# Requests for three of the four w_in pieces moved behind the first parting of the queries

## The chip, the cores and the metric

The kernel runs on one core of one Trainium2 chip. The metric is the device time of one execution in microseconds (us); lower is better. A time is the median of several executions. A profile is one more execution, recorded by the hardware profiler, with times counted from the start of its span.

## What is computed

Two blocks follow one another. The first is a gated linear attention with 4 batches, 8 heads, 768 tokens and 48 numbers a head. The second is a feed-forward block on 3072 tokens of width 384, with a hidden width of 1024, a softmax-weighted activation and a layer norm.

```python
for t in range(S):
    state = alpha[:, :, t, :, None] * state + np.einsum('bhd,bhe->bhde', k[:, :, t], v[:, :, t])
    y[:, :, t] = np.einsum('bhd,bhde->bhe', q[:, :, t], state)
...
h = x @ w_in
e = np.exp(h - h_max)
solu = h * (e / (np.sum(e) + 1e-09))
ln = (solu - mean) / np.sqrt(var + 1e-06) * g_ln
return ln @ w_out
```

The two weight matrices w_in (384 x 1024) and w_out (1024 x 384) arrive as 64-bit floats. The kernel brings their raw words into SBUF and makes 32-bit floats of them itself.

## The kernel before, in words

The tokens are worked on in six groups of 128 tokens of each of the four batches. For each group there is an attention part (turn alpha, keys and queries so that a head's numbers lie on partitions; scan alpha for the decays; scale keys and queries; scores; mask; read the values into y) and a feed-forward part (eight slices of the hidden width: `up_mm`, L390 to L398, multiplies x by a slice of w_in into a tile h; `up_act`, L400 to L413, takes the exponential on ScalarE, the product on VectorE and a square on ScalarE; `down`, L507, multiplies by w_out).

The schedule is written out by hand: every engine executes its instructions in the order in which the program text issues them. From the second group on, attention and feed-forward work of neighbouring groups are interleaved. The change is in the stretch ahead of that, which prepares group 0 (L674 to L780) and has no earlier group to lie beside.

What is issued there, by queue:

- **SP (SyncE)** requests by DMA, in this order: alpha (L674), k and q (L682, L683), each in two DMAs of 384 KB made of rows of 192 bytes; v (`load_v`, L173) in four of 192 KB; then w_in. The later w_out, k, q and alpha requests of the loop at L753 follow on the same queue. SP's requests share a fixed set of completion semaphores, so that a request can wait for the landing of the one eight places earlier.
- **w_in** comes in four pieces of 256 columns. `fetch` (L573 to L589) issues three DMAs a call, one for each 128 rows of w_in (L584). `fetch(0, 3)` brings the first piece (three of 256 KB) into slot 3 of the tile `room`, `fetch(1, 4)` the second (three of 256 KB) into slot 4, and `fetch(2, 1, 2)` the third and fourth together (three of 512 KB) into slots 1 and 2. `room` is 9216 columns wide, in six slots of 1536; later the products u and w_out pieces use it too.
- **VectorE (DVE)** turns a piece into 32-bit floats in five steps (`bit`, L613 to L636; the last, L636, writes w_in or w_out). The first piece is converted behind the masks of group 0 (`bits(0)`, L739), the second at L744, the third and fourth and all of w_out in the loop at L753, between the products at L409.
- **ScalarE** copies turned tiles, checks the raw pieces (`in_range`, L596 to L607) and parts the queries: `apart` (L243) takes the queries' last 16 dimensions, which lie in pairs of heads, and writes them twice, once multiplied by a column `parity` that is 1 on the even head's rows and once by its opposite. These are two instructions (L245), the first for even heads, the second for odd ones.
- **TensorE** turns alpha, k and q by matmuls with the identity (L164), computes the scores (`scores`, L271, matmuls at L278), in two halves of four heads; within a half first the first 32 dimensions of its heads, then the last 16 of the even heads, then those of the odd ones, which need the second instruction of `apart`. DVE (L289) and ScalarE with GpSimd (L297, L298) mask them. `read_values` (L356, matmuls at L333) then reads the values into y, batch after batch; ScalarE copies y to x (L363); `keys_back` (L300, L303) turns the keys back; and the loop at L753 begins with the first h (L394). `warm` (L449) fills TensorE with idle matmuls at the start and while q is awaited.

`apart` has three callers: L731 for group 0, L811 for group 1, and L899 for the others.

Of the kernel before, what the change touches and what calls it, by code (L numbers as in the profile page):

```python
# [32 lines left out]
def fast_path(ctx, tc, q, k, v, alpha, moe_w_in, moe_w_out, moe_g_ln, out):  # L33
# [12 lines left out]
    nc = tc.nc  # L46
# [34 lines left out]
    parity = const.tile([P, 2], FP, name="parity")  # L81
# [9 lines left out]
    slots = [room[:, 1536 * i : 1536 * i + 1536] for i in range(6)]  # L91
# [123 lines left out]
    def scan_on(g, i):  # L215
        part = slice(NP * i, NP * i + NP)
        scan(aT[:, part], aT[:, part], seed[:, part], False)
# [22 lines left out]
        copy(out=qe[:, :, P:SW], in_=h4[:, H:NB, 1:2])  # L240
        copy(out=qv[:, 0:H, P:SW], in_=h4[:, 0:H, 1:2])

    def apart():  # L243
        for i in range(2):
            nc.scalar.mul(  # L245
                out=qv[:, H : 2 * H, 0:P].rearrange("p (j i) t -> p j i t", i=2)[:, :, i], in_=qe[:, :, 0:P],
                mul=parity[:, i : i + 1],
            )
# [22 lines left out]
    def scores(g, half, a=None):  # L271
        a = a or banks("a", [NP, P])
        for last in range(2):
            for i in (0, 2, 1, 3):
                h = half * NP + i
                kb, qb = (H + h // 2, H + h) if last else (h, h)
                for b in range(B):
                    nc.tensor.matmul(  # L278
                        a[b][:, i], lhsT=kT[quarter(b), kb], rhs=qv[quarter(b), qb, 0:P], start=not last and not i, stop=bool(last),
                        tile_position=(32 * b, 0), skip_group_check=True,  # L280
                    )
        masks[half] = a
# [290 lines left out]
    def fetch(i, slot, n=1):  # L573

        kind, f = pieces[i]
        w = n * F // (2 if kind else KC)
        raw = room[:, 1536 * slot : 1536 * (slot + n)].bitcast(U32).rearrange("p (c f w) -> p c f w", f=w, w=2)
        if kind:
            parts = [(slice(0, P), c, moe_w_out[(f + c) * P : (f + c + 1) * P, :]) for c in range(2)]
        else:  # L580
            parts = [(slice(0, P), c, moe_w_in[c * P : (c + 1) * P, f * P : f * P + w]) for c in range(KC)]
        for rows, c, src in parts:
            if float64:
                nc.sync.dma_start(out=raw[rows, c].rearrange("p f w -> p (f w)"), in_=src.bitcast(U32))  # L584
            else:
                dst = w_out[rows, f + c, 0:DM] if kind else w_in[rows, c, f * P : f * P + w]
                nc.sync.dma_start(out=dst, in_=src)
        for m in range(n):
            raws[i + m] = raw[:, :, w // n * m : w // n * (m + 1)]  # L589
# [101 lines left out]
    nc.gpsimd.memset(kg, 0.0)  # L691
    load_v(0)
    fetch(0, 3)
    fetch(1, 4)
    fetch(2, 1, 2)
    nc.vector.memset(ones, 1.0)
    nc.vector.memset(small_ones, 1.0 / 32)
    nc.vector.memset(mhalf, -0.5)
    nc.vector.memset(w_out[:, :, DM : DM + 1], 1.0)

    def three(name, where):
        return [pool.tile([P, NP, P], FP, tag=tag, name=f"{name}{i}") for i, (pool, tag) in enumerate(where)]
# [20 lines left out]
    for i in (0, 2, 1):  # L723
        if i == 1:
            scan_on(0, i)
        part = slice(NP * i, NP * i + NP)
        nc.vector.tensor_tensor(
            out=qe[:, :, 0:P] if i == 2 else qv[:, part, 0:P], in0=t[i], in1=aT[:, part, 1:SW], op=ALU.mult
        )
        if i == 2:  # L730
            apart()  # L731
    scores(0, 0)
    t = [x.tile([P, NP, P], FP, tag=n, name="a_" + n) for x, n in ((ps_h, "h"), (ps_o, "o")) for _ in range(2)]
    scores(0, 1, t)
# [74 lines left out]
    scan_on(1, 2)  # L809
    nc.vector.tensor_tensor(out=qe[:, :, 0:P], in0=tq[2], in1=aT[:, H:NB, 1:SW], op=ALU.mult)  # L810
    apart()  # L811
    ends_of_decay()
    move_lasts()
# [56 lines left out]
    def attend(a, what):  # L870
# [19 lines left out]
        elif what == "firsts":  # L890
# [5 lines left out]
            if more:  # L896
                load(q, qn, a + 1)
        elif what == "apart":
            apart()  # L899
        elif what == "decay":  # L900
            decay(a)
# [89 lines left out]
    def compare(out, x, bound, op):  # L991
# [6 lines left out]
        out=chunks[:, :, 2], in0=sums[:, :, 2], scalar=0.25, in1=sums[:, :, 3], op0=ALU.mult, op1=ALU.is_le  # L998
# [6 lines left out]
    else:  # L1005
# [9 lines left out]
        out=bad, in0=all_ok[0:1, 0:1], scalar1=float(P * ends[-1]), scalar2=None, op0=ALU.is_lt  # L1015
# [415 lines left out]
def kernel(tc, *args):  # L1431

    with ExitStack() as ctx:
        taken = fast_path(ctx, tc, *args)
    with tc.If(taken > 0):
        general_path(tc, *args)
# [30 lines left out]
```

## Time and profile before

| | us |
|---|---|
| three executions without profile, median | 366.96 (366.78 to 367.19) |
| the profiled execution | 368.38 |
| its span, first to last instruction | 366.6 |
| TensorE busy in the span | 358.0 |
| VectorE busy | 243.9 |
| ScalarE busy | 146.5 |
| GpSimd busy | 130.3 |

The granted TensorE clock was 0.998. Of the 366.6 us, the first 28 us prepare and read group 0; the first h starts at 29.64, and from about 97.6 us on attention and feed-forward work alternate.

How to read the views. The page names an engine's busy time and its share of the span; a line of forty digits gives the busy tenths of forty equal slices. In timeline rows the columns are start, length, engine, line, operation, output and inputs, shape, count, and in brackets the idle time just before with what ended it; "issue" means that the profile shows nothing that the instruction waited for. A table of waits gives for each instruction and releaser the total, the number of times and the longest. A table of stretches gives for each stretch its length, busy time and instructions of TensorE's matmuls, TensorE's weight loads, VectorE, ScalarE and GpSimd, then the granted clock, the DMA share and GB/s. In DMA views q1 is the queue of SP's requests and q8 a queue of kind "instruction". A 32-bit matmul appears as two records, each with a weight load of its own.

The main times of the stretch that the change touches:

| what | start, us |
|---|---|
| SP requests v, four DMAs | 11.36, 12.87, 13.63, 15.24 |
| SP requests the first piece of w_in | 16.26, 16.94, 17.42 |
| SP requests the second piece | 17.90, 18.37, 18.85 |
| SP requests the third and fourth | 19.35, 21.11, 21.73 |
| scores of the first half begin | 17.73 |
| the two instructions of `apart` | 18.31, ending 19.65 |
| first y matmul | 22.26 |
| DVE's first conversion step, first piece | 24.15 |
| the same, second piece | 28.56 |
| first h | 29.64 |
| DVE's first conversion step, third piece | 33.66 |
| next SP request (w_out) | 31.58 |

### The profile page before, as it was taken

Reading aid. Unit: us, or ns where it says so; the run is one execution under the profiler, and the core shown is the slowest. Engines: PE = TensorE matmul, PEld = TensorE weight load, DVE = VectorE, ACT = ScalarE, POOL = GpSimd, SP = SyncE. Lnnn points to the kernel's source line nnn. Section 1 sums busy time; section 2 is a strip of 40 time slices with the busy share of each in tenths; the row PEclk is TensorE's granted clock in tenths of the full one; section 3 lists DMA queues with packets and bytes.
Section 4 is the critical chain, followed back from the end, with each engine's and each line's share of the span. In section 5 each row is a group of like instructions: output and inputs, shape, how many; then the busy total and the mean of one; then the engine's idle time right before and its main releaser. Section 6 shows DMA issues by size and latency. Waiting matters only on the chain. (4 is left out here: it accounts for less than half of the span.)

```text
span 366.6 us, 10041 instructions
## 1 busy us (share of the span) xinstructions
PE 358.0 (98%) x4341; PEld 216.0 (59%) x4341; DVE 243.9 (67%) x375; ACT 146.5 (40%) x262; POOL 130.3 (36%) x127
## 2 busy tenths in 40 slices
PE   8989999999999999999999999999999999999994
PEld 8866345666655566556475556575556565555552
DVE  0999989979997796936665946766946404445420
ACT  3637887372736261252531253531242222222110
POOL 7020000003368663764232763332773121233300
PEclk9999999999999999999999999999999999999999
DMA  9994997326196509354044454004042000000011
GB/s 178 186 333 139 194 302 156 88 59 146 68 222 133 131 4 192 90 123 123 5 108 92 103 115 113 21 25 88 21 96 66 0 25 1 23 21 22 23 46 51
DMA packets 72871, 36.06 MB, mean 98 GB/s; under 512 B 48232, under 2 KB 70000, under 8 KB 72816
## 3 DMA queue, kind: packets, MB, share of 16 engines
q1 hardware_dynamic: 71792, 34.39, 39.6%
q10 hardware_dynamic: 1024, 0.92, 0.8%
q8 instruction: 36, 0.59, 0.7%
q14 instruction: 19, 0.16, 0.1%
HBM read 25.30 MB, written 4.72 MB: 82 GB/s over the span
## 5 line engine op out<-in xcount | busy, mean ns | idle before, releaser
L513 PE MATMUL o<-w_out,room 128*128 128x385 f32 x384 | 133.8, 491 | 0.0
L394 PE MATMUL h<-x,w_in 128*128 128x512 f32 x288 | 131.6, 597 | 0.0
L513 PEld LDWEIGHTS o<-w_out,room 128*128 128x128 f32 x384 | 71.1, 189 | 55.2 <-issue 13.4
L394 PEld LDWEIGHTS h<-x,w_in 128*128 128x128 f32 x288 | 53.2, 189 | 58.0 <-issue 49.0
L409 DVE TENSOR_TENSOR room<-h,e 128x512 f32<-128x512 f32 x40 | 27.6, 690 | 72.7 <-ACT e L408 72.7
L408 ACT ACTIVATE e<-h 128x512 f32<-128x512 f32 x40 | 23.9, 598 | 98.9 <-PE h L394 98.9
L427 POOL TENSOR_TENSOR p<-p,e 128x512 f32<-128x512 f32 x30 | 43.1, 1437 | 20.3 <-ACT e L408 20.2
L412 ACT ACTIVATE u<-room 128x512 f32<-128x512 f32 x40 | 25.2, 630 | 37.0 <-DVE room L409 37.0
L552 POOL TENSOR_TENSOR r<-sums,mhalf 128x1 f32<-128x1 f32 x20 | 14.8, 740 | 67.9 <-DVE sums L543 67.7
L289 DVE TENSOR_TENSOR sT<-a,mask 128x512 f32<-128x512 f32 x43 | 26.7, 682 | 8.7 <-PE a L278 8.7
L204 DVE TENSOR_TENSOR_SCAN hT<-aT,unit 128x516 f32<-128x516 f32 x18 | 24.3, 1396 | 7.9 <-ACT aT L709 7.8
L204 DVE TENSOR_TENSOR_SCAN aT<-aT,seed 128x516 f32<-128x516 f32 x18 | 25.4, 1441 | 0.2
L225 POOL TENSOR_TENSOR kT<-kT,hT 128x1024 f32<-128x1024 f32 (+1 forms) x8 | 13.3, 1687 | 33.6 <-DVE kT L179 33.6
L278 PEld LDWEIGHTS a<-qv,kT 32*128 32x128 f32 x704 | 21.1, 186 | 6.8 <-issue 2.4
L427 DVE TENSOR_TENSOR p<-p,u 128x512 f32<-128x512 f32 x30 | 21.7, 723 | 5.1 <-ACT u L412 5.1
L333 PE MATMUL y<-sT,vn 128*32 128x128 f32 x768 | 23.3, 274 | 1.6 <-issue 1.4
L278 PE MATMUL a<-qv,kT 32*128 32x128 f32 x704 | 23.7, 279 | 0.2 <-ACT qv L245 0.2
L212 POOL COPY fend<-hT 128x12 f32<-128x12 f32 x6 | 3.0, 507 | 56.4 <-DVE hT L204 56.4
L333 PEld LDWEIGHTS y<-sT,vn 128*32 128x32 f32 x768 | 20.9, 110 | 3.5 <-issue 2.7
L196 ACT ACTIVATE sq<-an,mone 128x1536 uint8<-128x1536 f32 x12 | 18.9, 1572 | 0.2
L554 ACT ACTIVATE o_sb<-o,r 128x384 f32<-128x384 f32 x16 | 9.3, 580 | 18.5 <-POOL r L552 18.5
L261 POOL TENSOR_TENSOR state<-state,lot 128x384 f32<-128x384 f32 x10 | 8.8, 902 | 15.6 <-DMA lot<-qv 15.6
(150 smaller groups left out, 376.7 us busy)
## 6 DMA issues: line engine op xcount, KB each, us to landing
vn<-in_v_dram SPq DMA_DIRECT2D x24, 192.0 KB, 4.7
an<-in_alpha_dram SPq DMA_DIRECT2D x20, 192.0 KB, 4.0
out_dram<-o_sb SPq DMA_DIRECT2D x20, 192.0 KB, 1.9
room<-in_moe_w_out_dram SPq DMA_DIRECT2D x8, 384.0 KB, 5.6
kn<-in_k_dram SPq DMA_DIRECT2D x16, 192.0 KB, 4.8
qn<-in_q_dram SPq DMA_DIRECT2D x16, 192.0 KB, 3.8
lot<-qe SPq DMA_DIRECT2D x40, 64.5 KB, 2.1
lot<-qv SPq DMA_DIRECT2D x20, 129.0 KB, 2.4
```

What stands on the lines that cost most here:

```text
L196: nc.scalar.activation(out=sq, in_=x, func=AF.Relu, scale=sign, bias=mone, accum_out=over[:, g, i : i + 1])
L204: nc.vector.tensor_tensor_scan(out=o, data0=a, data1=s, initial=1.0, op0=ALU.mult, op1=ALU.add)
L278: nc.tensor.matmul(a[b][:, i], lhsT=kT[quarter(b), kb], rhs=qv[quarter(b), qb, 0:P], start=not last and not i, stop=bool(last), tile_posit ...
L289: nc.vector.tensor_tensor(out=sT[:, b, half * NP : half * NP + NP], in0=a[b], in1=mask[:, None, :].to_broadcast([P, NP, P]), op=ALU.mult,)
L333: nc.tensor.matmul(y_bank(b)[quarter(r), a], lhsT=lhsT, rhs=rhs, start=(b, r) not in begun, stop=stop, tile_position=(row, 32 * r), skip_g ...
L394: nc.tensor.matmul(h, lhsT=w_in[:, a, f * P : (f + 1) * P], rhs=d["x"][:, a].rearrange("p b t -> p (b t)"), start=(a == 0), stop=(a == KC ...
L408: nc.scalar.activation(out=e, in_=h, func=AF.Exp)
L409: nc.vector.tensor_tensor(out=u, in0=h, in1=e, op=ALU.mult)
L412: nc.scalar.activation(out=u2, in_=u, func=AF.Square)
L427: eng.tensor_tensor(out=p, in0=d[0][i] if f == 1 else p, in1=d[f][i], op=ALU.add)
L513: nc.tensor.matmul(d["o"][:, 0 : DM + 1], lhsT=u_of(g, f)[:, b * P : b * P + P], rhs=w_out[:, f], start=(f == 0), stop=(f == FC - 1), skip ...
L552: nc.gpsimd.tensor_tensor(out=r, in0=s[:, 3:4], in1=mhalf, op=ALU.pow)
```

## The change

`fetch(1, 4)` and `fetch(2, 1, 2)` are taken from behind `fetch(0, 3)`. They are put into a function `fetch_more`, which first writes one column of slot 4 by a copy on ScalarE, and which `apart` calls for group 0 between its two instructions. The second piece's DMAs write the same slot, so SP's requests for it are held until that copy is done; those for the third and fourth pieces follow behind them in SP's order. The column is overwritten by the piece. The other two calls of `apart` stay as they were.

```diff
-    def apart():
+    def apart(between=None):
         for i in range(2):
+            if i and between:
+                between()
             nc.scalar.mul(
...
     fetch(0, 3)
-    fetch(1, 4)
-    fetch(2, 1, 2)
     nc.vector.memset(ones, 1.0)
...
+    def fetch_more():
+        nc.scalar.copy(out=slots[4][:, 0:1], in_=parity[:, 0:1])
+        fetch(1, 4)
+        fetch(2, 1, 2)
...
         if i == 2:
-            apart()
+            apart(fetch_more)
     scores(0, 0)
```

## The prediction

> **What bounds the kernel now.** I read the page first. TensorE is busy for 98% of the span, at full clock:
>
> ```profile
> PE 358.0 (98%) x4341; PEld 216.0 (59%) x4341; DVE 243.9 (67%) x375; ACT 146.5 (40%) x262; POOL 130.3 (36%) x127
> PE   8989999999999999999999999999999999999994
> q8 instruction: 36, 0.59, 0.7%
> ```
>
> So only what makes TensorE start its unbroken stretch earlier, or what breaks it, can move the end. Second, the table of waits for TensorE alone, up to 110 us:
>
> ```profile
> PE y L333 <- issue: 1.4, 1, 1.4
> PE warm L452 <- DVE ones L696: 1.1, 1, 1.1
> PE tp_k L164 <- DMA kn<-in_k_dram: 0.5, 1, 0.5
> ```
>
> The longest wait is 1.4 us, inside the first reading of values, and it has no releaser. Third, the timeline around it:
>
> ```profile
> 23.09 0.64 PE L333 MATMUL y<-sT,vn 128*32 128x128 f32 x14 [0.20 <-DVE sT L289]
> 25.15 3.04 PE L333 MATMUL y<-sT,vn 128*32 128x128 f32 x102 [1.41 <-issue]
> 28.27 1.53 PE L303 MATMUL tp<-ident,kT 128*128 128x128 f32 x12
> 29.64 2.74 PE L394 MATMUL h<-x,w_in 128*128 128x512 f32 x6
> ```
>
> TensorE stops at 23.74 in the middle of batch 0, between two matmuls with the same operands' tiles, and goes on at 25.15. After that I found no gap above 0.04 us. What is missing at 23.74 is code: the stop comes after 957 records (36 warm, 3 x 96 turning, 128 scores and 26 y matmuls, as many weight loads, and one load more). The page has 8682 records on TensorE and 36 packets on q8, 241 records for each packet of 16 KB. The DMA view cut to a sliver at 22.65 to 22.72 holds one such packet; it starts at 22.68 and takes 0.97, and none is seen between 13.55 and then. TensorE resumes 1.50 us after it ends. Fourth, the table of stretches says what else the DMA engines did:
>
> ```profile
> 18.00:20.50 2.50, 2.32 (x72) 2.02 (x72) 2.16 (x4) 1.34 (x2) 0.00 (x0) 1.00 0.90 173
> 20.50:22.70 2.20, 2.20 (x76) 2.00 (x72) 2.19 (x4) 0.81 (x2) 1.27 (x1) 1.00 1.06 385
> 23.70:25.20 1.50, 0.09 (x6) 0.05 (x5) 1.47 (x3) 0.00 (x0) 0.78 (x2) 1.00 1.03 399
> 27.70:30.00 2.30, 2.30 (x33) 1.92 (x24) 2.26 (x4) 1.60 (x5) 0.00 (x0) 1.00 0.07 29
> ```
>
> The last two columns are DMA share and GB/s: the engines are full, with v and then w_in, from before 18 until 27.7 us.
>
> **What the Trainium skill says.** "Runtime: NRT & Kernel Launch", Instruction fetch mechanics: instructions come in 16 KiB blocks of 256, by a DMA queue that the sequencer drives itself while it executes the current block, and crossing a boundary is mostly hidden. The trace agrees on size and number (16 KB, 241 records each); here one crossing is not hidden. "DMA: Bandwidth & Descriptors", Queues, rings and completion order: each DMA engine takes turns between its queues, a packet of descriptors at a time. If that were all, a fetch would hardly wait; the trace has it waiting. The last block before was begun near record 445, at 13.3, with its fetch at 13.55; 256 records later TensorE is at 18.4 (it decodes some way ahead, so 17.9 to 18.4), and the next fetch begins at 22.68, 4.3 us or more late.
>
> **The change, part by part.** *Removed from 17.90 to 22.06:* six of the nine w_in requests of SP. *Added:* one ScalarE copy of a column between the two multiplications by parity (L245, 18.31 to 19.65, the first ending near 18.98). *Moved:* the six requests to behind that copy. No other SP request lies between the old and the new place; the next one on SP is the w_out request at 31.58. POOL's queue is not touched.
>
> The copy: the nearest row is the one-column activation of L676, 203 ns. Bounds: 0.1 (the two multiplications overlap by 0.1) to 0.25 with the semaphore update it carries; I take 0.2. Queued behind it is the second multiplication, for which the odd heads' scores wait (TensorE had 19.70 there), then the first copy of scores on ScalarE and the masks of DVE, which start at 20.45 on the end of those scores. So TensorE and DVE both run 0.2 later from here. In the present trace that is covered: TensorE's by the 1.41 stall, DVE's by its idle 0.28 at 33.05:
>
> ```profile
> 33.05 0.69 DVE L409 TENSOR_TENSOR room<-h,sT 128x512 f32<-128x512 f32 x1 [0.28 <-ACT sT L408]
> 46.17 0.69 DVE L409 TENSOR_TENSOR room<-h,sT 128x512 f32<-128x512 f32 x1 [0.20 <-ACT sT L408]
> 49.67 0.69 DVE L409 TENSOR_TENSOR room<-h,sT 128x512 f32<-128x512 f32 x1 [0.36 <-ACT sT L408]
> 50.73 0.57 DVE L622 TENSOR_SCALAR lot<-room 128x768 uint32<-128x768 uint32 x1 [0.37 <-DMA room<-in_moe_w_out_dram]
> ```
>
> Without cover it costs up to 0.2.
>
> The requests: the fourth w_in request of SP started at 17.90 and now starts near 19.3, 1.4 later. The ninth starts at 21.73 because it waits for the first one's landing (21.72), so it moves to 22.0 at most. The first piece (0.79 MB) alone takes 2.0 us at 385 GB/s, so engines that began it at 18.2 are fed until 20.2 or, at the slow rate of 18 to 20.5, until 21. A request needs about 1.0 us to its first packet (0.74 to 1.7 for alpha): 20.3. So the engines hardly run dry, and the end of w_in moves by 0 to 0.8 (27.7 to at most 28.5). The second piece landed at 26.58 and is read by DVE at 28.56: slack 2.0. The last landed at 30.33 and is read at 33.66: slack 3.3. Delaying them costs nothing.
>
> The stall: when TensorE asks for its block, nothing but v and the first piece is now ahead or about to be. To remove the stall the packet must start at 23.74 - 0.97 - 1.50 = 21.27 or earlier, 1.4 earlier than now. Bounds for what it gains: 0 (it waits for v and the first piece only, and did before) to all 1.41. I take all.
>
> What is late next: with the 0.2 of the copy TensorE would end y 1.21 earlier, turn the keys back and reach the first h at 28.43. But h also needs the first piece converted by DVE (L636, ending 28.48, now 28.68), so it starts near 28.80 in place of 29.64: **0.84 gained**. Then the loop runs as before: TensorE ran without a gap, and of its waits on DVE the nearest (two buffers of h) have 0.1 to 1 us in hand. At 79.06 the scores of the second group need the last queries, and DVE finishes them only at 78.92:
>
> ```profile
> 78.23 0.69 DVE L817 TENSOR_TENSOR qv<-tp_q,aT 128x512 f32<-128x512 f32 x1
> 79.06 2.07 PE L278 MATMUL a<-qv,kT 32*128 32x128 f32 x64
> ```
>
> So DVE must come 0.84 earlier as well. From 29 to 79 it idles 0.28 + 0.14 + 0.16 + 0.20 + 0.36 + 0.37 = 1.51 us in waits that TensorE, ScalarE or DMA set; less the copy's 0.2 and some 0.2 that any hand-over keeps, 1.1. The last of them waits for w_out, whose requests follow, on SP, the check of the first piece on ScalarE (31.57), which follows the keys' copies and so TensorE: it comes earlier too. So 0.84 passes through to the unbroken stretch behind 79 us.
>
> The sum: the profiled execution took 368.38 us, 366.6 of it span; it would take 368.38 - 0.84 = 367.54. The runs without profile have a median of 366.96, 1.42 less; there I forecast 366.96 - 0.84 = **366.1**. A difference of about 0.2% (0.73 us) is what a measurement can tell from no change; the forecast lies just beyond.
>
> **Rivals.** *The fetch isn't helped* (0.30). The first three requests landed 5.5, 5.5 and 5.8 us after 16.26, 16.94 and 17.42: at 21.7, 22.4 and 23.2; the fourth, asked for at 17.90, only 7.3 later at 25.2. The even step is 0.67, so the slowest engine put some 1.3 us of something else between third and fourth, where the fetch with its 0.97 lies. Then the fetch waited for v and the first piece, which stay where they are, and deferring the rest changes nothing; the copy's 0.2 hides under the stall: 366.95. Against it: the run shown is one, and the fetch is asked for within 0.5 us of the fourth request, so in other executions it may come behind it. The same time results if SP isn't held at all.
>
> *Part of the stall goes* (0.07): gains of 0.2 to 0.6, 366.4 to 366.75.
>
> *The second piece comes late* (0.11), the other side. If the DMA engines run dry and start as slowly as from 18 to 20.5 (173 for 385 GB/s, which loses 1.4 us), with the 1.4 of the request the second piece lands 2.8 late, and over 2.0 late DVE waits at 28.56, and after another 0.28 (its idle time at 33.05) everything up to 79.06 does. At 3.2 late: 3.2 - 2.28 = 0.92 lost, 367.9. Against it: v and the first piece keep the engines fed to about 21.
>
> **How the numbers follow.** Stall gone 0.52 (of it 0.02 inside 0.2%, as the cap of 0.84 lies so close), not helped 0.30, partly 0.07, late piece 0.11. Faster 0.50, same 0.39, slower 0.11. The range: down to 366.96 - 1.3 = 365.7, all that DVE's idle time lets through without the copy's cost; up to 366.96 + 0.2 = 367.15, a copy without cover. It leaves out the late piece and a little below: some 0.15.
>
> **What would show it.** Right: no wait on "issue" in y near 24, the 16 KB packet before 21.3, first h near 28.8, DVE's waits at 46 to 50 shorter, scores at 78.2. Wrong: y still resumes near 25.15; or DVE waits for w_in at 28.6; or scores of the second group stay at 79.06, DVE having kept its times.

## The result and the profile after

| | before, us | after, us |
|---|---|---|
| median, 22 executions each | 366.94 (366.62 to 367.61) | 367.36 (366.61 to 369.92) |
| the profiled execution | 368.38 | 367.35 |
| its span | 366.6 | 365.6 |
| first 16 KB packet after 20 us starts | 22.68 | 20.93 |
| first h starts | 29.64 | 28.64 |

The ratio of the times, after to before, is 1.0018 with a 95% interval of 1.0009 to 1.0026: the change makes the kernel slower, by about 0.2%. The forecast was 366.1, and 367.36 lies above the range too.

The two profiled executions say the opposite: 1.0 us gained. The page of the changed kernel shows the same work:

```profile
span 365.6 us, 10044 instructions
PE 358.0 (98%) x4341; PEld 216.2 (59%) x4341; DVE 243.2 (67%) x375; ACT 146.8 (40%) x263; POOL 129.4 (35%) x127
```

In its timeline of TensorE the stop on "issue" in y is gone: the first row below is y, all 116 matmuls of it in one piece, where before 14 and 102 stood with 1.41 between them.

```profile
23.11 3.47 PE L335 MATMUL y<-sT,vn 128*32 128x128 f32 x116 [0.20 <-DVE sT L291]
26.66 1.53 PE L305 MATMUL tp<-ident,kT 128*128 128x128 f32 x12
28.64 2.81 PE L396 MATMUL h<-x,w_in 128*128 128x512 f32 x6 [0.45 <-DVE g_col L650]
```

The timeline of ScalarE has the added copy (L702) between the two multiplications: 0.17 us, of which 0.09 is beside the first.

```profile
18.32 0.72 ACT L247 ACTIVATE qv<-qe,parity 128x512 f32<-128x512 f32 x1 [2.87 <-DVE qe L732]
18.95 0.17 ACT L702 COPY room<-parity 128x1 f32<-128x1 f32 x1
19.03 0.72 ACT L247 ACTIVATE qv<-qe,parity 128x512 f32<-128x512 f32 x1
```

So in this pair the forecast's signs came (the scores of the second group start at 78.13, where 79.06 stood and 78.2 was forecast), and yet the medians go the other way. Two things in the numbers ask for a cause. First, the profiled execution of before took 368.38, and none of the 22 executions of before beside the change took over 367.61. Second, of the 22 executions of after seven took over 368.0, up to 369.92, while the quickest (366.61) is as quick as before's (366.62). The fastest executions are as fast as before; what differs is the tail of long ones.

The table of stretches shows one lasting difference, in DMA. For after, the row whose counterpart in before had a DMA share of 0.07 and 29 GB/s:

```profile
27.70:30.00 2.30, 1.85 (x8) 0.93 (x7) 2.27 (x4) 2.27 (x7) 0.00 (x0) 1.00 0.49 191
```

w_in now ends about 0.8 later (last 4 KB packet done at 30.71, before 29.90), and what used to be a quiet stretch is half full.

### The profile page after: what moved, and what is told of

It reads as the page before. It is cut to its first block, busy times and chain, and to the rows that moved or that the text cites. A ratio compares the mean times of both kernels' runs of the same rounds, so it can differ in the third digit from the quotient of the medians.

```text
span 365.6 us, 10044 instructions
## 1 busy us (share of the span) xinstructions
PE 358.0 (98%) x4341; PEld 216.2 (59%) x4341; DVE 243.2 (67%) x375; ACT 146.8 (40%) x263; POOL 129.4 (35%) x127
## 5 line engine op out<-in xcount | busy, mean ns | idle before, releaser
L429 POOL TENSOR_TENSOR p<-p,e 128x512 f32<-128x512 f32 x30 | 42.2, 1406 | 20.3 <-ACT e L410 20.2
```

Of the source, the lines that this page charges most:

```text
L429: eng.tensor_tensor(out=p, in0=d[0][i] if f == 1 else p, in1=d[f][i], op=ALU.add)
```

## The experiments

Three theories were to be told apart. **C**: the copy itself costs something in ScalarE's order. **D**: the third piece of w_in comes too late for its first reader. That reader is ScalarE's range check (L606), at 31.99 in after; VectorE's first step comes only at 33.27 there (33.66 before). **F**: the delayed w_in traffic delays TensorE's own next instruction blocks, the 16 KB packets on q8. The expectations below, written before the runs, use these letters. They also call two blocks by number, and so does the text: the "fifth" is the one whose 16 KB packet starts near 28 us in before and after, the "sixth" the one whose packet comes next, between 30.9 and 35.6. These are names only: in the profiles the two are the fourth and fifth packet of q8. Ratios are to the kernel before on the same chip.

**Both kernels again** (ctl_before, ctl_after; ctl_after2 on another chip). No edit.

> The kernel before, once more, for its spread and a second profile. Theory A (before's usual execution has no fetch stall, and the 1.4 us stall belonged to the one profiled execution): the profile has a span near 365.2, no wait on issue near 24 us, first h near 28.6. Theory B (the stall is there in every execution of before, and the change pays elsewhere): span near 366.6 again, y resuming near 25.1. Times 366.6 to 367.6 in either.

> The changed kernel, once more. Its times should again be spread from 366.6 to about 370, with a median of 1.001 to 1.003 of before. Theory F (some executions wait for a block of instructions that comes in late behind the moved requests): if the profile falls on a long one, TensorE has a wait on issue of 1 to 3 us between 23 and 35 us. Theory D (late w_in): instead DVE waits for the second or third piece near 28.5 or 33. Theory C (the copy): no such wait, a constant 0.1 to 0.4.

> The changed kernel a third time, for more executions and one more profile beside the three that follow. A seventh to a third of its executions above 368 us, up to 372, the rest like before.

ctl_before: 367.13 (366.69 to 367.79), ratio 1.0003 [0.9994, 1.0011]. ctl_after: 366.98 (366.69 to 371.99), 1.0011 [0.9993, 1.0029], with three of 22 at 369.24, 371.57 and 371.99. ctl_after2: 367.51 (366.80 to 370.75), 1.0016 [1.0000, 1.0032], with three of 14 over 368. Each of these two intervals reaches 1; with the first comparison all three lie on the slower side. The tail came back on both chips. More telling is the profile of ctl_before, 367.00 us with a span of 365.2. First its timeline of TensorE:

```profile
22.89 3.67 PE L333 MATMUL y<-sT,vn 128*32 128x128 f32 x116 [0.20 <-DVE sT L289]
28.41 2.81 PE L394 MATMUL h<-x,w_in 128*128 128x512 f32 x6 [0.24 <-DVE g_col L648]
```

This is the kernel before, unchanged, and it has no stop in y: its packet started at 21.17, and its first h at 28.41, 1.23 earlier than in the execution that the forecast was made from. Two more profiles with the requests at their old place (copy_only and kv_later_b below) have no stop in y either: what the change was to remove isn't there in a usual execution. The other way round, ctl_after2 and look_b, of the changed kernel, had a stop of 0.56 in y each, with their packets at 21.70 and 21.58. In seven profiles of the changed kernel (with look_a to look_d below) the packet starts between 20.54 and 21.70, in the middle 21.07; in the three other profiles with the requests at their old place (ctl_before, copy_only, kv_later_b) at 21.17, 21.05 and 21.15. The change does not even move it.

The table of stretches of ctl_before, on the other hand, agrees with the first profile of before:

```profile
27.70:30.00 2.30, 2.06 (x9) 1.10 (x8) 2.16 (x5) 2.27 (x7) 0.00 (x0) 1.00 0.08 29
```

The quiet stretch is a property of the kernel before, the stop in y is not.

**The copy alone** (copy_only), the requests at their old place:

```diff
     fetch(0, 3)
+    fetch(1, 4)
+    fetch(2, 1, 2)
...
-        nc.scalar.copy(out=slots[4][:, 0:1], in_=parity[:, 0:1])
-        fetch(1, 4)
-        fetch(2, 1, 2)
+        nc.scalar.copy(out=mean_sb[:, 0:1], in_=parity[:, 0:1])
```

> The copy alone, into a column that is written again later; the requests stand where they stood before. Theory C: 1.0005 to 1.0015 of before, with before's narrow spread. Theories F and D: within 1.0005 of before, and no executions above 368.

366.97 (366.69 to 368.09), ratio 0.9997 [0.9987, 1.0007]. One of 13 lay above 368, by 0.09, where none was expected. C falls: the copy costs nothing that can be measured.

**Only the third and fourth piece held** (gate34):

```diff
     fetch(0, 3)
+    fetch(1, 4)
...
-        nc.scalar.copy(out=slots[4][:, 0:1], in_=parity[:, 0:1])
-        fetch(1, 4)
+        nc.scalar.copy(out=slots[1][:, 0:1], in_=parity[:, 0:1])
         fetch(2, 1, 2)
```

> Only the third and fourth pieces are held behind the copy; the second is requested where it was before. Theory F with the second piece as what matters: like before, no executions above 368. Theory F with the end of w_in as what matters (a fetch behind all of it): like the changed kernel, a spread up to 370. Theory D with the second piece late: like before.

367.01 (366.59 to 367.63), ratio 0.9997 [0.9989, 1.0006]. Three held requests in place of six cost nothing that can be measured. None of 13 was above 368.0; at the 13 of 62 that the plain change shows in all, that would happen by chance about once in twenty times, so the absence of a tail is not firm here. Its DMA share from 27.7 to 30.0 was 0.33, between before and after. Its profile, though, shows a wait of 0.36 on "issue" inside the h of the second slice, at 35.28, a place where the forecast had looked for nothing.

**The hold made longer** (late2): the six requests behind a later instruction of ScalarE, so that they start at 21.2 in place of 19.2.

```diff
-            apart(fetch_more)
+            apart()
...
-        masked_apart(half, B - 1)
+        masked_apart(half, B - 1, None if half else fetch_more)
```

> The copy and the requests one step later, behind ScalarE's first copy of scores, near 21.2 us. All of w_in comes some 2 us later, so that what is only sometimes late now is late always. Theory D (ScalarE's range check of the third piece, near 32 us, waits for the last landing, and ScalarE's exponentials wait behind it): a wait of ScalarE of 1 us or more at the check, 1.002 to 1.006 of before. Theory F (a block of TensorE's instructions comes in behind w_in): a wait on issue of 1 us or more in TensorE between 28 and 36 us. Theory D2 (the second piece): DVE waits near 28.5.

369.45 (367.19 to 371.48), ratio 1.0064 [1.0039, 1.0089]. Here the tail has become the rule, and a profile shows it. The waits of TensorE, and its timeline at the longest:

```profile
PE h L398 <- issue: 1.9, 1, 1.9
```

```profile
32.83 2.41 PE L398 MATMUL h<-x,w_in 128*128 128x512 f32 x5
37.17 3.16 PE L398 MATMUL h<-x,w_in 128*128 128x512 f32 x7 [1.92 <-issue]
```

TensorE stops behind the fifth h of the second slice, between matmuls of the same tiles, with no releaser in the profile: the same picture as the stop in y, at another block. The 16 KB packet for it started at 34.62, and TensorE resumed 2.55 later; in the first profile of before it was 22.68 to 25.15, 2.47. The stretch before it is full in this kernel:

```profile
27.70:30.00 2.30, 1.84 (x8) 0.91 (x7) 2.25 (x4) 2.27 (x7) 0.00 (x0) 1.00 0.99 394
```

And SP's own requests that follow are w_out (two) and keys (two), at times that the hold hardly moves (w_out 29.95 in after):

```profile
29.91 0.80 SPq L588 DMA_DIRECT2D room<-in_moe_w_out_dram  x2
30.81 3.65 SPq L146 DMA_DIRECT2D kn<-in_k_dram  x2
```

But D has something to show in this profile as well: ScalarE's check did wait for its piece.

```profile
32.80 0.91 ACT L608 ACTIVATE sq<-room 128x768 f32<-128x768 f32 x1 [0.77 <-DMA room<-in_moe_w_in_dram]
```

**That check taken out of the way** (check_later on the change, late2_check on late2): the first range check of the third piece one slice later.

```diff
-    checks = {0: [(2, 0)], 1: [(2, 1)], 2: [(3, 0)], 3: [(3, 1)], 4: [(1, 0), (1, 1)], 5: [(4, 0), (4, 1)]}
+    checks = {1: [(2, 0), (2, 1)], 2: [(3, 0)], 3: [(3, 1)], 4: [(1, 0), (1, 1)], 5: [(4, 0), (4, 1)]}
```

> The changed kernel with the first step of the third piece's range check done one slice later, behind 35 us; nothing else moves. Theory D: no executions above 368.2, median of before. Theory F: the long executions stay, a seventh to a third of them above 368.

> The later hold, with the first step of the third piece's range check one slice later, so that ScalarE no longer waits for the last landing. Theory D: back to 1.000 to 1.002 of before. Theory F: 1.005 to 1.008 as with the later hold alone, TensorE's wait on issue near 35 us stays at 1.5 us or more.

check_later: 367.27 (366.85 to 371.12), ratio 1.0021 [1.0004, 1.0038], four of 13 over 368. late2_check: 369.55 (366.81 to 371.35), ratio 1.0045 [1.0024, 1.0065]. The tail stays in both (12 of 17 above 368.0 in late2_check): D falls as its cause. Whether the check adds a little in late2 is open, as the two intervals of late2 and late2_check overlap. The profile of late2_check was a long execution (370.38), and its timeline of TensorE shows three waits on "issue", 3.30 us in all:

```profile
24.12 3.04 PE L337 MATMUL y<-sT,vn 128*32 128x128 f32 x102 [0.53 <-issue]
...
32.59 1.55 PE L375 MATMUL kv<-vn,kg 128*32 128x48 f32 x123 [1.02 <-issue]
...
38.23 2.31 PE L398 MATMUL h<-x,w_in 128*128 128x512 f32 x5 [1.75 <-issue]
```

Three blocks in a row came late: their packets started at 21.77, 30.18 and 35.60, and TensorE resumed 2.35, 2.41 and 2.63 later. With usual starts of 27.4 to 28.0 and 30.9 to 32.7 where w_in isn't held (ctl_before, copy_only, kv_later_b), the second was 2 to 3 us late and the third 3 to 5.

**The hungry step moved** (kv_later on the change, late2_kv on late2, kv_later_b on before): `next_state(0)`, whose 128 short matmul records kv take 1.57 us and use up 256 records with their weight loads, more than the 241 that a packet brings on average, from the first slice of the loop to the third.

```diff
         if f == 0:
-            next_state(0)
             fetch(4, 3)
...
         elif f == 2:
+            next_state(0)
             ends_k = ends_of(kn, "e")
```

> The changed kernel with the 256 TensorE instructions of the first state update done two slices later, so that the block of instructions fetched near 28 us is needed some 2.5 us later. Theory F with that block: no executions above 368.2. Theory D: the long executions stay.

> The later hold (behind ScalarE's first copy of scores), with TensorE's first state update two slices later, so that the sixth block of its instructions is needed near 37 us and not near 35. Theory F (the loss is TensorE waiting for that block): of the 2.4 us that the later hold loses at least 1.5 come back, 1.0000 to 1.0025 of before, and no wait on issue above 0.5 us near 35. Theory D (the third piece's landing, through ScalarE's check): stays at 1.005 to 1.008.

> The kernel before with the first state update two slices later: what that move is worth by itself. No effect of its own expected, 0.9990 to 1.0008 of before; if before's executions between 367.4 and 368.4 come from the same wait for a block, its highest time falls below 367.6.

kv_later: 367.19 (366.80 to 367.95), ratio 1.0006 [0.9998, 1.0014], none of 13 over 368 (by itself as weak as gate34's none). late2_kv: 367.08 (366.60 to 368.10), ratio 0.9998 [0.9986, 1.0009]; late2 alone had 1.0064. Three of 14 are above 368.0, none above 368.10, where late2 had seven of eight. On before the edit is worth nothing, 1.0005 [0.9995, 1.0016] (its highest, 368.47 and 368.50, are above the 367.6 that was expected). The timeline of late2_kv:

```profile
28.38 7.96 PE L398 MATMUL h<-x,w_in 128*128 128x512 f32 x18 [0.44 <-DVE g_col L652]
36.27 1.57 PE L375 MATMUL kv<-vn,kg 128*32 128x48 f32 x128
```

Eighteen h in one piece, then kv without a wait, although w_in is still late: DMA share 0.91 from 27.7 to 30.0 and last 4 KB packet done at 31.41, against 0.99 and 32.24 in late2 and 30.71 in after. In this one profile the fifth and sixth packets also came earlier than in late2 (27.64 and 32.50, against 28.93 and 34.62), so that the fourteen times weigh more than the trace. The w_in requests and the check are those of late2; what moves is kv, and with it ScalarE's two copies of kv into the state (L383, 34.23 in late2, 40.03 here). Since late2's long wait is one of TensorE with no releaser in the profile, those copies aren't what it waited for. The move gives the whole 0.64% back in the median and decides for F against D.

**The keys' requests ahead of w_out's** (late2_kfirst on late2), to see whether it is the crowd of requests from 30 us on in which the block is late:

```diff
-            fetch(4, 3)
             load_first(k, kn, 1)
+            fetch(4, 3)
             load_first(q, qn, 1)
```

> The later hold, with the next group's k requested ahead of the two w_out requests and not behind them. Theory F with w_out's packets of 3 KB as what the sixth block stands behind: its fetch comes before 33.5 us where it came at 34.6, the wait on issue near 35 shrinks below 1.0 us, 1.001 to 1.004 of before. If the rest of w_in holds the block back, nothing changes: 1.005 to 1.008.

369.74 (368.41 to 370.89), ratio 1.0074 [1.0054, 1.0095]. The sixth packet came at 32.57 in place of 34.62 and the wait at 35 shrank from 1.92 to 0.11, which fits F. But the time did not fall, against the 1.001 to 1.004 expected; in the profiled execution a new wait stands in its place. TensorE's timeline at 70 us:

```profile
69.65 1.14 PE L517 MATMUL o<-w_out,room 128*128 128x385 f32 x3
72.17 1.08 PE L164 MATMUL tp_q<-ident,u 128*32 128x128 f32 x32 [1.38 <-DVE kT L804]
```

The swap moved more than an order: the keys' requests start at 24.65 in place of 30.81, and those of w_out at 32.62 in place of 29.91. Why the turning waits for kT here and not in late2 was not found; the run supports F at the one place and settles nothing about the total.

**The change itself in further profiled executions** (look_a to look_d), to catch a long one. No edit.

> The changed kernel once more, for one profiled execution, to catch one of its long executions (13 of 58 so far were above 368.0). If this execution lies above 368.0, theory F (late instruction blocks) expects a TensorE wait put down to issue of at least 0.8 us, between 31 and 39 us, with the fifth or sixth 16 KB packet starting at least 1.0 later than in an execution near 367.0, and no wait of that size for a landing of w_in or for VectorE. Theory D (a late third piece) expects a wait for w_in's landing of that size instead. If it lies near 367.0, F expects the sixth packet to start by about 33.2 and at most 0.4 of wait there.

> As the look before it: above 368.0, F expects an issue wait of at least 0.8 us between 31 and 39 us behind a late fifth or sixth 16 KB packet, D a wait for w_in's landing; near 367.0, the sixth packet starts by about 33.2 with at most 0.4 of wait.

> As the two looks before it: above 368.0, F expects an issue wait of at least 0.8 us between 31 and 39 us behind a late fifth or sixth 16 KB packet, D a wait for w_in's landing; near 367.0, the sixth packet starts by about 33.2 with at most 0.4 of wait.

> As the three looks before it: above 368.0, F expects an issue wait of at least 0.8 us between 31 and 39 us behind a late fifth or sixth 16 KB packet, D a wait for w_in's landing; near 367.0, the sixth packet starts by about 33.2 with at most 0.4 of wait.

They took 367.46, 367.27, 367.76 and 367.18: none above 368.0, so what was expected of a long execution was not put to the test. But the longest of the four has the mark. The timeline of look_c:

```profile
32.66 2.41 PE L396 MATMUL h<-x,w_in 128*128 128x512 f32 x5
36.02 4.45 PE L396 MATMUL h<-x,w_in 128*128 128x512 f32 x10 [0.95 <-issue]
```

The same place as in late2, now in the plain change. Its packet started at 33.68; the DMA view cut to 33.60 to 33.75 (queue, kind: packets, MB, share of the 16 engines) shows in what company:

```profile
q1 hardware_dynamic: 177, 0.04, 114.5%
q8 instruction: 1, 0.02, 38.7%
```

In 0.15 us 177 small packets of the keys' request are under way beside the one block. In after, ctl_before, look_a, look_b and look_d the packet starts among w_out's packets of 3 KB. The sixth packet in look_a to look_d started at 33.30, 33.01, 33.68 and 32.89, and the waits at 35 were 0.09, 0.25, 0.95 and 0.09 (in look_a, where TensorE came 0.5 later by itself, 33.30 was early enough). Over all profiles with a wait there (gate34, check_later, look_b, look_c, late2, late2_check) TensorE resumed 2.33 to 2.63 after the packet's start. It needs its block at about 35.2, so the packet must start by about 32.8 (an estimate: 35.2 less 2.4). Over the seven profiles of the changed kernel it starts between 31.44 and 33.68, in the middle at 32.89. In the three with both the requests and kv at their old place it started at 31.12 (before), 30.90 (copy_only) and 32.69 (ctl_before, with a wait of 0.09): once with nothing in hand and twice with time to spare. So the block comes later in the changed kernel, but the two sets overlap, and they are few.

## Why the prediction was wrong

**"The stall", wrong: taken as a property of the kernel.** The 1.41 at 23.74 belonged to the one profiled execution. The text had the sign of it in hand: that execution took 368.38, "1.42 less" the median of the runs shown, whose highest was 367.19. The difference was noted and then not explained. In every later profile the time exceeds the span by the same 1.7 to 1.9, in long executions and short ones, so the 1.42 was not a cost of profiling. It was the stop itself: remove 1.23 of first-h delay from 368.38 and one is at 367.15, a usual time. The step "366.96 - 0.84" took off a loss which the median never had. Of the fetch's "4.3 us or more" of delay, most is there without a stop too: the packet starts at 21.05 to 21.17 in the three other profiles with the requests at their old place, 2.6 to 2.8 us behind TensorE's record 701, the point that the prediction counted from.

**"Nothing but v and the first piece is now ahead", not shown.** In the profiled execution the packet did come 1.75 earlier. But over the profiles it starts in the middle at 21.07 with the requests held and at 21.05 to 21.17 without, so the early packet can't be credited to the hold. This is the rival "the fetch isn't helped", for a reason which it didn't give: it was seldom late. Its price, no change, is what the quick executions show.

**"The end of w_in moves by 0 to 0.8 ... Delaying them costs nothing", size right, price wrong.** It moved 0.8 in the first pair (29.90 to 30.71; the forecast's 27.7 was the end of the full stretch and not of w_in). Over all profiles it is 29.18 to 29.90 with the requests at their old place, 30.21 to 30.71 in the changed kernel. The slack was counted for data only, and there with the wrong reader for the third piece (VectorE at 33.66; ScalarE's check reads it at 31.99). The reader that mattered isn't in a list of tiles at all: TensorE's sequencer, which needs its fifth block five matmuls into kv (by about 31.4) and its sixth by 35.2. The prediction put the hold's cost on the loop behind the first h at nothing; there it brought long executions, and 0.25 and 0.95 of wait for the sixth block in look_b and look_c. Holding six requests fills the quiet stretch from 27.7 (0.07 or 0.08 to 0.49 in the first pair, 0.30 to 0.67 over the seven profiles), and the sixth block then comes in among w_out's and the keys' packets. The rival "the second piece comes late", the one for the slower side, had the sign, the wrong transfer and the wrong victim.

**What was right.** The copy: 0.17 measured, 0.2 taken, and without a cost that can be measured (copy_only, 0.9997 [0.9987, 1.0007]). For the profiled pair, the arithmetic behind the stop: first h at 28.64 (28.80 forecast), 367.35 in place of 368.38 (367.54 forecast). That this pair agrees with the forecast is luck: ctl_before, with no edit at all, shows the same gain (first h at 28.41, 367.00).

**How the size comes out.** Of 62 executions of the changed kernel in all comparisons 13 took over 368.0, of 162 of the kernel before 6 did. The medians of the two are 367.20 and 367.06, the means 367.61 and 367.14. Nearly all of the 0.46 between the means is the tail: the executions up to 368.0 alone have means of 367.13 and 367.10; the difference of medians in a comparison of 22 depends on how many long ones fall in it.

**What stays open.** The longest execution of the plain change seen in a profile lost 0.95 at this place. That those of 369 to 372 are the same with one or two more blocks late is argued from late2_check (3.30 in three waits) and from kv_later, which has none of them. That a later fifth block is what makes the request for the sixth late is argued too: in look_c the fifth started at 27.96 and the sixth only at 33.68, in look_d at 27.78 and 32.89, so the company the sixth meets seems to count as well. No view shows when TensorE's sequencer asks for a block, so how much of a late start is a late request and how much is waiting behind other packets stays open.

## What to carry to other kernels

Before a gap in a profile is worth removing, hold the profiled execution's own time against the runs: if it lies outside their range by about the gap's size, the gap is likely that execution's alone, and one more profile of the same kernel tells. When a transfer is delayed, list what else will be on the DMA engines at the new time, and put the engines' own instruction blocks on the list of readers, above all around steps of many short matmuls. A change whose quickest executions stay the same can still cost time by its tail.

## What the runs showed of the hardware

- A block of instructions that comes late stops TensorE: 1.41 us (before), 1.92 (late2), 1.02 and 1.75 (late2_check), 0.95 (look_c). "Runtime: NRT & Kernel Launch" of the Trainium skill, Instruction fetch mechanics, calls the crossing "mostly hidden". In the usual executions here it is, and full DMA engines alone don't change that: in ctl_before they were full (share 1.00 from 20.50 to 22.70) when the packet of 21.17 started, and y had no stop. The waits above show that it isn't always.
- From the start of the 16 KB packet to the first matmul out of it 2.3 to 2.6 us passed in the fourteen such waits of 0.19 us or more ahead of 40 us, the packet itself taking 0.9 to 1.1 of it. That the time is so even is the best sign that these stops are waits for the block.
- kv uses up 256 records in 1.57 us, and the wait fell five h behind it, about 3.8 us after kv began. The same number of records lasts many times as long in h or o, where the page of before has 597 and 491 ns for one matmul. So the need for blocks is as uneven as the mix of matmuls, which no view of busy time shows.
